# A prime-factor transform in place of the direct one, in a fused attention and long-convolution kernel

## The chip, the cores and the metric

The kernel runs on one NeuronCore of a Trainium2 chip. Such a core has five engines that run side by side, each with its own queue of instructions: TensorE (matrix products, here PE, with its weight loads PEld), VectorE (DVE), ScalarE (ACT), GpSimd (POOL) and SyncE (SP), which here only issues DMA transfers. The engines wait for each other by semaphores. Products land in PSUM, a small memory of eight banks of 512 fp32 words for each of 128 partitions; everything else lies in SBUF. The metric is the device time of one execution in microseconds (us).

## What is computed

Attention with a mask that differs by head, then a gated long convolution over the sequence, and a projection. Cut to what matters:

```python
B, H, S, D = 4, 8, 768, 64          # after attention: x is 4 x 768 x 512
scores = np.matmul(q, k.transpose(0, 1, 3, 2)) / 8
a = softmax(where(mask, scores, -1e9))   # heads 0, 2, 6: causal; the others: causal, and
                                         # the last 64 positions or the first 4 keys
x = (a @ v), heads side by side
proj = x @ w_proj                   # 512 -> 3 * 512
x1, x2, x3 = three parts of proj
X2 = rfft(x2, n=S); Hf = rfft(filter_fft, n=S)
y = x1 * irfft(X2 * Hf, n=S) * x3   # a circular convolution along the 768 positions
out = y @ w_out
```

The transform along the sequence is linear, so the kernel transforms the attention's output first and projects its spectrum with the middle third of w_proj. A real transform of 768 points has 385 frequencies; the kernel holds them as cosine and sine rows and computes all of it by matrix products with tables.

## The kernel before

**Tiling.** A pair of heads (128 columns of x) is one unit, n = 0 to 15; four pairs make a batch, b = 0 to 3. A sequence of 768 is six tiles of 128 positions.

**An order written out by hand.** Every step is a small function with a name, registered by `@op(name)`. The strings AHEAD and FAST list the names in the order in which they are issued; since each engine takes its instructions in order, the strings set the order on every engine. A name can carry an engine (`/v` VectorE, `/s` ScalarE, `/p` GpSimd, for copies and two-input steps that more than one can do) and a PSUM bank (`@0` to `@7`). Two helpers write these steps: `ev` (lines 969 to 975) copies, `two` (line 978) combines two operands; so in the profile most copies have one line and are told apart by their tiles.

**The steps of one pair n.** `lq`, `lk`, `lv` load; `cq`, `ck`, `cv` cast to bf16; `T`, `E` turn q and k (by TensorE and a copy for n below TURNED = 8, by a DMA transpose above); `kx`, `ks`, `vx`, `vs` gather the few keys and values that a windowed head needs; `sc` the scores (line 1452); `ex` the exponentials on ScalarE (line 1471, tile pT). The mask is added to the scores by TensorE, as a product of an identity with a table of large negative numbers, for n below BIASED_FAST = 4 (`sb`, line 1465), and multiplied into the exponentials by VectorE or GpSimd otherwise (`mk`, `mr`, table mtab). `at` multiplies with the values (line 1516), `rec` and `nm` divide (line 1533), into tile attn. `tn` and `te` turn attn into xT (channels on partitions), by TensorE for the pairs in TURNED_BACK and by a DMA transpose for the others.

**The forward transform of a pair.** `fd` and `fe` form the difference and the sum of the two halves of the sequence (tile fo): odd and even frequencies. For the pairs in SIXTHS (all of them) `fA`, `fS`, `fb`, `fr` split each half once more by three (tiles uv, br). `W{n}.{u}` (lines 1569 to 1573) is then three products for each u, of 256, 256 and 128 columns, into bank u; `We{n}` copies both banks (2 x 384 words) to xh.

**The filter.** Its columns are folded (`fold0`, `fold1`), transformed by `F` (line 1265, 18 products of 512 columns with the tables G and Gh) and scaled into HAB by `H` steps, with two DMA transfers `Hd` that move rows between partition halves. The tables come from one sine and one cosine over 384 columns (`sin`, `cos`), mixed by `skew` and `Gm` steps; the inverse table Gi is the forward table turned by TensorE (`Gt`, line 1227, and `Ge`).

**The middle, per batch b.** `X{b}.{t}.{u}` projects the spectrum (line 1620), `Xe` copies it out, `pa`, `pb`, `pc` multiply it with the filter as complex numbers into tile P (t = 0 to 2). For t = 2 the two DMA transfers `sw` swap partition halves first (tile Xw).

**The inverse and the gates, per block cb of 128 channels.** `x1` and `x3` project x itself (line 1655), `xs` copies x1 out, `g` multiplies with x3 straight from PSUM (line 1674; for the last cb line 1678) into tile gy. `c{b}.{cb}.{r}` is the inverse: for r = 0 and 1 three products of 384 columns (line 1685). `ce` copies the first to evs, `cv{b}.{cb}.0` and `.1` add and subtract the second (line 1696) into conv, 768 positions, and `y` multiplies conv into gy. `o` projects (line 1712), `oe` copies out, `st` stores: two tiles of 128 positions at a time (512 KB), one at a time in the last batch.

**Warm-up.** `blank` steps are products of zeros, in 13 places of the first part (BLANKS counts them).

The reuse of memory is set by hand too: a tile's tag says which it shares, and RAW gives sizes. A general version for other head patterns follows behind a branch that isn't taken.

Of the kernel before, what the change touches and what calls it, by code (L numbers as in the profile page):

```python
# [9 lines left out]
FP32 = mybir.dt.float32  # L10
# [111 lines left out]
lflag lk0 lq0 lk1 lq1 mblank want tcol fcol0 table sin0 fcol1 blank0@6 tfrac quarter mtab0 par turns other angle  # L122
ident mtab1 wrap size sin cos
# [3 lines left out]
ones1 ones2 mtab3 blank5@0 lq2 lk2 blank10@1 ck0/v skew0/s lv0 parb skew1/p G32/s T0.1@2 xp0 cq0/v lk3 blank6@3  # L127
mtab2 E0.1/v lv1 blank8@4 Gk1/s lv3 blank7@5 Gm00 btab G31/p blank1@6 ck1/v kz1 lq3 T0.0@7 lk4 alt blank3@0 Gm2
cq1/s G30/p Gh0 lq4 T1.1@1 Gm01 kz0 lv2 E0.0/s G00/v T1.0@3 G01/p Gm1 cq2/s lk6 E1.1/v sc0.1@4 sb0.1 lq6 ck2/p
sc0.3@6 ex0.1 Gh1 E1.0/v sc0.4@0 ones0 kx1/p sb0.4 lk5 sb0.3 T2.1@2 ex0.4 kz2 lk7 sc0.0@4 E2.1/v lq5 cv0/p sb0.0  # L130
Gt1@3 ex0.3 lq7 blank2@0 kx2/v Gt2@1 Gk0/p ex0.0 lv6 T2.0@2 ks1/p Ge2/v ck3/p sc0.2@6 Ge1/s E2.0/v sc1.2@4 sb1.2
lfilt sb0.2 T3.1@0 ex1.2 sc0.5@2 Gt0@1 ex0.2 cv1/v sc2.3@4 E3.1/v lv4 vx1/p sb0.5 ex0.5 sc1.0@6 lw2.1 Ge0/v
sb1.0 ks2/s vs1/v at0.0@2 lw2.0 ex1.0 at0.1 cq3/v lw0.1 T3.0@0 ex2.3 kx3/v sc1.1@6 rec0 lw1.1 sb1.1 nm0/v cv3/s
blank11@1 ex1.1 sc2.1@4 fe0/p sb2.1 tn0@1 cq4/v E3.0/s at1.0@2 lw0.0 blank9@6 ex2.1 ks3/v sc2.4@6 ck4/v at1.1
lw1.0 ex2.4 T4.0@0 T4.1@4 vs3/v E4.0/s te0/v lwo sc3.1@6 sb3.1 rec1 E4.1/s nm1/v fd0/p sc3.2@0 sb3.2 ex3.1 fe1/v
tn1@5 fS0/p ex3.2 sc3.0@2 fold0/v sb3.0 sc2.0@6 ex3.0 vx3/v fd1/v F0.0@4 fA0/v fA1/p F0.1@0 H0.0/s fS1/v fb0/p
sb2.0 fold1/v sc2.2@2 H0.1/s sb2.2 ex2.0 fb1/p te1/v F1.0@1 fr1 ex2.2 F2.1@4 fr0 cv2/v H1.0/s F2.0 lv5 vs2/v
vx2/p H0.2/v at2.0@6 H2.0/s at2.1 ck6/p sc4.0@2 H2.1/s rec2 Hd0 at3.0@0 nm2/v at3.1 H2.2/s lk9 rec3 fe2/p F1.1@6
nm3/v ex4.0 Hd1 T6.1@7 fd2/p H1.1/v sc4.5@4 sc4.4@0 ex4.5 tn2@2 fe3/v ex4.4 fd3/v tn3@3 te2/v sc4.2@4 te3/v
ex4.2 mk4.2/p W1.0@0 E6.1/v W1.1 blank4@2 We1/s ks6/v sc4.1@4 fS3/p blank12@3 ex4.1 fA3/v sc4.3@0 fr3 x10.3.0@2  # L140
fb3/p cq6/s mk4.0/v W0.0@4 W0.1 ex4.3 lq9 x10.3.1 ck7/v ck5/s x30.0.0@0 We0/v fS2/p lk10 kx6/s T7.1@7 cq5/p
xs0.3/s x10.0.1@4 H1.2/s fA2/v lq8 x10.0.0 fb2/v E7.1/s fr2 mk4.1/v W3.0@2 lk8 cq7/s T5.0@6 xs0.0/v ks7/p
x30.0.1 E5.0/s lq10 kx7/v W3.1 cv6/v T7.0@7 We3/s T5.1@4 vs6/v lv9 vx6/p g0.0 T6.0@5 E7.0/s W2.1@2 W2.0 E6.0/v
cv4/p E5.1/s x10.1.0@0 We2/v kx5/s ks5/p lv7 at4.0@6 sc5.1@4 cv5/s sc5.0@2 H2.3 at4.1 H2.4 ex5.1 lv8 vx5/p
x10.1.1 rec4 vs5/p nm4/v ex5.0 sc5.2@4 ex5.2 sc6.0@6 H2.5 sc6.3@2 mk5.1/v ex6.0 X0.0.1@4 mk5.0/v mk5.2/v ex6.3
X0.0.0 mk6.0/v fe4/v xs0.1/s fd4/v sc7.1@6 sc6.1@2 fS4/v Xe0.0/s fA4/v sc7.0@0 fr4 ex6.1 pa0.0/v at5.0@4 at5.1
fb4/v mk6.1/p ex7.0 X0.1.1@2 rec5 nm5/v X0.1.0 ex7.1 fe5/v mk7.0/v X0.2.1@0 cq8/s fd5/v mk7.1/v Xe0.1/s sc7.2@4
sc6.4@6 X0.2.0 fA5/p ex7.2 ck10/v sc6.2@2 pa0.1/v Xe0.2/s tn4@4 pb0.1/v tn5@5 ex6.2 sw0.1 W4.0@0 mk7.2/v W4.1
sw0.0 ck8/v x10.2.0@2 We4/s pc0.1/v T8 cq10/s mr6/v x30.1.0@0 mk6.2/v ck9/s x30.1.1 fS5/v pa0.2/v T10 ex6.4
x10.2.1 fb5/p g0.1 cv7/s at6.0@6 cq9/s vx7/v x30.2.1@0 te5/v xs0.2/s fr5 T9 x30.2.0 vs7/v cv8/s W5.1@2 pb0.2/v  # L150
W5.0 te4/s at6.1 lk12 pc0.2/v We5/s lq11 rec6 pb0.0/p g0.2 c0.1.0@5 cv9/s c0.0.0@4 lk13 nm6/v sc8.2@2 ce0.0/s
sc8.4@0 ex8.2 lv10 ce0.1/v c0.2.0@4 pc0.0/v sc8.1@6 ex8.4 lk11 sc8.0@2 ks10/v fe6/v c0.1.1@5 vx9/v ex8.0 lq13
vs9/v c0.0.1@0 cv0.1.1 c0.3.1@1 ks9/p ex8.1 lq12 cv0.1.0 kx9/p sc8.3@2 y0.1/v c0.3.0@5 ex8.3 lv11 cv0.0.1
mk8.0/p at7.1@6 ce0.3/s cv0.0.0 at7.0 lv12 sc8.5@2 cv0.3.1 ce0.2/s tn6@0 ex8.5 y0.0/v x30.3.0@4 kx10/s rec7
mk8.2/p cv0.3.0 nm7/s x30.3.1 te6/v sc10.3@2 mk8.1/v y0.3/v at8.0@0 fd6/v g0.3 fS6/p at8.1 ck13/p tn7@6 ex10.3
rec8 sc10.1@4 te7/v c0.2.1@7 fe7/p ex10.1 x11.0.0@2 fA6/v fd7/p cv0.2.0 x11.0.1 cv0.2.1 x11.3.1@4 fb6/p xs1.0/s
# [772 lines left out]
def patterned(tc, pools, pre, q, k, v, flags, n_sink, window, moe_w_proj, moe_filter_fft, moe_w_out, out):  # L929
# [912 lines left out]
```

## Time and profile before

| | us |
|---|---|
| three runs | 190.65, 190.84, 192.29 |
| median | 190.84 |
| the profiled execution | 190.27 |
| its span, first to last instruction | 188.4 |
| VectorE busy in the span | 161.2 |
| ScalarE busy in the span | 145.6 |
| GpSimd busy in the span | 69.0 |

The time of an execution is a little longer than the span of its profile. A line of the profile with groups gives the source line, engine and operation, what was written from what with its shape, the count, the busy time in us and the mean ns of one, and after the last bar the idle time of the engine just before them with what ended it. A chain of waits goes back from the last instruction, at each step to what released it. TensorE's granted clock was 0.985 of full speed in the mean. The DMA queues moved 34.01 MB, most of it before 124 us.

### The profile page before, as it was taken

How to read it: one execution, taken by the hardware profiler on the slowest of the kernel's cores; microseconds unless marked ns; L12 is line 12 of the kernel's file. 1: busy time of each engine (PE TensorE's matmuls, PEld its weight loads, DVE VectorE, ACT ScalarE, POOL GpSimd, SP SyncE). 2: the span in 40 equal slices, each digit the busy share in tenths (PEclk: the TensorE clock that was granted, in tenths of full speed). 3: DMA queues.
4: the chain of work that ended last, by engine and by line, in shares of the span. 5: the costliest groups of instructions: out<-in, count | busy, mean ns of one | idle time of the engine just before them, and what ended most of it. 6: DMA issues, size and time to landing. Idle time of an engine off the chain costs nothing.

```text
span 188.4 us, 4493 instructions
## 1 busy us (share of the span) xinstructions
PE 176.5 (94%) x1694; PEld 103.4 (55%) x1694; DVE 161.2 (86%) x329; ACT 145.6 (77%) x210; POOL 69.0 (37%) x103
## 2 busy tenths in 40 slices
PE   7879999989998999999999999999999999999970
PEld 2437664647745563575555656655657765555530
DVE  6887799789889999999989999999899996499810
ACT  5787899999999999988989999696977332426360
POOL 5874785554322224670250460700650630000000
PEclk9978999999999999999999999999999999999997
DMA  4999999999999999999999989982162002312074
GB/s 152 330 274 279 208 197 236 270 286 251 213 202 225 215 185 166 233 219 213 202 233 228 228 221 238 250 87 56 60 98 111 3 2 111 135 36 111 11 286 157
DMA packets 78955, 34.01 MB, mean 180 GB/s; under 512 B 68306, under 2 KB 75218, under 8 KB 78930
## 3 DMA queue, kind: packets, MB, share of 16 engines
q1 hardware_dynamic: 75986, 30.81, 73.9%
q0 software_dynamic: 2944, 2.88, 9.1%
q8 instruction: 14, 0.23, 0.5%
q14 instruction: 11, 0.09, 0.2%
HBM read 24.64 MB, written 6.29 MB: 164 GB/s over the span
## 4 chain that ended last, share of the span: by engine, by line
PE 66%; ACT 14%; DVE 6%; DMA 5%; issue 3%; POOL 2%; SPq 2%; DVEq 0%; ACTq 0%; POOLq 0%
PE space L1655 18%; PE space L1712 11%; PE space L1620 8%; PE space L1452 7%; PE space L1685 7%; PE space L1516 6%; ACT f_pT L1471 4%; DMA f_qkT<-f_qk_bf 3%; ACT f_HAB L1274 3%; DMA f_v_f<-in_v_dram 2%; PE space L1465 2%; ACT f_qk_bf L975 2%; SPq L1383 2%; PE space L1569 1%; PE space L1571 1%
## 5 line engine op out<-in xcount | busy, mean ns | idle before, releaser
L1471 ACT ACTIVATE f_pT<-space 128x1024 bf16<-128x1024 f32 (+3 forms) x68 | 58.8, 917 | 6.1 <-PE space L1465 1.9
L1655 PE MATMUL space<-f_xT,f_wproj 128*128 128x384 bf16 x256 | 47.9, 326 | 0.1
L1655 PEld LDWEIGHTS <-f_wproj 128*128 128x128 bf16 x256 | 24.0, 98 | 17.1 <-issue 1.0
L1712 PE MATMUL space<-f_wout,r_gy 128*128 128x512 bf16 x96 | 24.7, 379 | 0.0
L1452 PE MATMUL space<-f_qkT 64*128 64x128 bf16 (+3 forms) x248 | 22.6, 253 | 1.1 <-DVE f_attn L1533 0.5
L1620 PE MATMUL space<-f_wproj,f_xh 128*128 128x512 bf16 x96 | 22.7, 379 | 0.1
L1685 PE MATMUL space<-f_Gi,r_P 128*128 128x384 bf16 x96 | 19.0, 326 | 0.7 <-ACT f_evs L975 0.3
L978 DVE TENSOR_TENSOR f_pT<-f_pT,r_mtab 128x1024 bf16<-128x1024 bf16 (+3 forms) x33 | 18.5, 583 | 0.8 <-ACT f_pT L1471 0.6
L975 ACT COPY f_o<-space 128x1024 f32<-128x1024 f32 (+1 forms) x12 | 9.9, 836 | 11.3 <-PE space L1712 11.2
L1516 PEld LDWEIGHTS <-f_pT 128*128 128x128 bf16 x472 | 16.7, 97 | 3.6 <-issue 0.9
L1516 PE MATMUL space<-f_v_aug,f_pT 128*128 128x65 bf16 x392 | 17.9, 193 | 0.6 <-ACT f_X L975 0.5
L1452 PEld LDWEIGHTS <-f_qkT 64*128 64x128 bf16 x248 | 10.3, 94 | 13.1 <-issue 10.4
L978 POOL TENSOR_TENSOR f_uv<-f_fo 128x256 bf16<-128x256 bf16 x12 | 9.1, 766 | 21.1 <-DVE f_fo L978 15.8
L1696 DVE TENSOR_TENSOR f_conv<-f_evs,space 128x384 bf16<-128x384 f32 x32 | 16.1, 545 | 0.6 <-PE space L1685 0.3
L975 ACT CAST f_xh<-space 128x768 bf16<-128x768 f32 x14 | 11.2, 808 | 4.9 <-PE space L1573 4.6
L1620 PEld LDWEIGHTS <-f_xh 128*128 128x128 bf16 x96 | 9.0, 98 | 10.0 <-issue 0.4
L1712 PEld LDWEIGHTS <-r_gy 128*128 128x128 bf16 x96 | 9.0, 98 | 8.9 <-issue 0.4
L1533 DVE TENSOR_TENSOR f_attn<-space,f_rec 128x768 bf16<-128x768 f32 x14 | 13.4, 955 | 0.4
L1685 PEld LDWEIGHTS <-r_P 128*128 128x128 bf16 x96 | 8.8, 97 | 7.4 <-issue 1.1
L978 POOL TENSOR_TENSOR f_fo<-f_attn 128x384 bf16<-128x384 bf16 x11 | 10.4, 960 | 2.4 <-DVE f_attn L1533 1.9
L975 ACT CAST f_X<-space 128x1024 bf16<-128x1024 f32 x8 | 8.2, 1020 | 2.8 <-PE space L1620 2.7
L978 POOL TENSOR_TENSOR f_pT<-f_pT,r_mtab 128x512 bf16<-128x512 bf16 (+1 forms) x6 | 6.8, 1146 | 9.1 <-ACT f_pT L1471 9.1
(136 smaller groups left out, 345.7 us busy)
## 6 DMA issues: line engine op xcount, KB each, us to landing
f_v_f<-in_v_dram SPq DMA_DIRECT2D x32, 192.0 KB, 4.7
out_dram<-f_o SPq DMA_DIRECT2D x9, 512.0 KB, 3.1
r_qk_f<-in_k_dram SPq DMA_DIRECT2D x10, 192.0 KB, 4.4
r_qk_f<-in_q_dram SPq DMA_DIRECT2D x10, 192.0 KB, 5.0
r_qk_f<-in_k_dram SPq DMA_DIRECT2D x4, 384.0 KB, 11.3
r_qk_f<-in_q_dram SPq DMA_DIRECT2D x4, 384.0 KB, 6.1
f_qk_f<-in_q_dram SPq DMA_DIRECT2D x4, 384.0 KB, 5.8
f_qk_f<-in_k_dram SPq DMA_DIRECT2D x4, 384.0 KB, 6.6
```

The lines of the kernel that those rows point to most:

```text
L975: nc.scalar.copy(out=out, in_=in_)
L978: (nc.gpsimd if now["engine"] == "p" else nc.vector).tensor_tensor(out, a, b, op)
L1274: nc.scalar.activation(out=out_(), in_=in_(), func=AF.Copy, scale=w / S)
L1452: nc.tensor.matmul(sc[:, bank, col:col + 128 * cnt], lhsT=keys, rhs=qkT(n)[rows, 0, 128 * i:128 * (i + cnt)], start=(col == 0 or not biase ...
L1471: nc.scalar.activation(out=pT(n)[:, c, :, 0:w], in_=held[f"sc.{n}.{c}"][:, :, 0:w], func=AF.Exp, scale=SCALE)
L1516: nc.tensor.matmul(att[:, hh, 65 * i:65 * i + 65], lhsT=pT(n)[:, c, bank, col:col + 128], rhs=values, start=(z == 0), stop=(z == len(here) ...
L1533: nc.vector.tensor_mul(attn(n).rearrange("p i hh d -> p hh i d"), rows[:, :, :, 0:64], held[f"rec.{n}"][:, :, :, None].to_broadcast([128, ...
L1620: nc.tensor.matmul(ps[:, u, :], lhsT=xh(b)[:, cc, chain, 128 * part:128 * part + 128], rhs=wproj()[:, cc, DM:2 * DM], start=(cc == 0), sto ...
L1655: nc.tensor.matmul(ps[:, s, 0:HS], lhsT=wproj()[:, cc, part * DM + cb * 128:part * DM + (cb + 1) * 128], rhs=xT(b)[:, cc, s * HS:s * HS + HS],
L1685: nc.tensor.matmul(ps[:, 0, 0:HS], lhsT=P(b)[:, t, u, ch], rhs=Gi()[:, tile_no], start=(m == 0), stop=(m == 2))
L1696: fn(conv[:, half * HS:half * HS + HS], held[f"evs.{b}.{cb}"], held[f"c_ps.{b}.{cb}.1"][:, 0, 0:HS])
L1712: nc.tensor.matmul(ps, lhsT=gy(b)[:, cb, i * 128:(i + 1) * 128], rhs=wout()[:, cb, :], start=(cb == 0), stop=(cb == NC - 1))
```

## The change

The transform is computed as 3 by 256 instead: 768 is 3 times 256, and the two are prime to each other, so the positions and the frequencies can be numbered by remainders and no mixing factors are needed between a transform of length 3 and one of length 256.

- **Forward.** `fe`, `fd`, `fA`, `fS`, `fb`, `fr` stay, with other signs and slots. `W` keeps three products per u of 256, 256 and 128 columns, but u = 0 and 1 now go into the same banks: u writes the words 2f + u, that is every second word. `We` then copies one row of 768 contiguous words; xh is six groups of 128.
- **Tables.** G has six tiles instead of 18. One sine and one cosine over 512 columns (five index steps on GpSimd, `fcol0` to `fcol4`). The inverse tables Gi and Gj are written directly; the turns `Gt`, their copies `Ge`, and the mixing steps go.
- **Filter.** It takes the pairs' way, in four blocks of 128 columns: `fAF` to `frF`, the half spectra `K{cc}.{u}`, copies `Ke{cc}`, then 24 turns by TensorE (`F0` to `F2`) and the scalings `H` into HAB. No `Hd`.
- **Middle.** No `sw`. Behind `pc`, nine steps per batch do the length-3 part of the inverse: `qa`, `qs`, `qz`, `qb`, `qp`, `qm` (two inputs, 1024 elements) and `qh`, `qd`, `qr` (scalings; `qr` 2048 elements on one partition).
- **Inverse.** `c{b}.{cb}` is six products of 256 columns, two for each remainder of the position by three. `ce` and the two half combinations go. For batches 0 to 2 (DIRECT) `y` multiplies straight from PSUM; for batch 3 `cv` copies first.
- **Positions by remainder.** `xs` and `g` read x1 and x3 from PSUM with a step of three words, so that gy is sorted by remainder; a row tile of the output is then every third position, and `st` stores such rows.
- **Masks as biases** for n below 8 instead of 4. **TURNED_BACK** loses n = 14. **BLANKS** has 21 products instead of 29. A step `gate` on GpSimd reads one element of pair 3's load ahead of the filter's and the weights' loads.
- AHEAD and FAST are a new order, with new banks and engines.

The diff, cut to its core (the order strings are left out):

```diff
-SIXTHS = (0, 1, 2, 3, 4, 5, 6, 7, 8, 9, 10, 11, 12, 13, 14, 15)
-TURNED_BACK = (0, 1, 2, 3, 4, 5, 6, 7, 14, 15)
+TURNED_BACK = (0, 1, 2, 3, 4, 5, 6, 7, 15)
-BIASED_FAST = 4
+BIASED_FAST = 8
-BLANKS = (5, 2, 2, 2, 2, 2, 2, 2, 2, 2, 2, 2, 2)
+BLANKS = (5, 2, 2, 2, 2, 2, 2, 2, 2)
+DIRECT = ((0, 0), (0, 1), (0, 2), (0, 3), (1, 0), (1, 1), (1, 2), (1, 3), (2, 0), (2, 1), (2, 2), (2, 3))
...
+    def spectrum(ps, u, uv, br, ch):
+        woven = lambda bank, count: ps[:, bank, 0:2 * count].rearrange("p (f u) -> p u f", u=2)[:, u]
+        nc.tensor.matmul(woven(0, 256), lhsT=br[:, 1, u, ch], rhs=G()[:, 3 * u:3 * u + 2], start=True, stop=False)
+        nc.tensor.matmul(woven(0, 256), lhsT=uv[:, 2 * u, ch], rhs=Gk()[:, u], start=False, stop=True)
+        nc.tensor.matmul(woven(1, 128), lhsT=br[:, 0, u, ch], rhs=G()[:, 3 * u + 2], start=True, stop=True)
+
+    def taken(x, ps):
+        ev(x.rearrange("p g f -> p (g f)"), ps.rearrange("p a f -> p (a f)")[:, 0:S])
...
-            ev(xh(b)[:, hp], held[f"W_ps.{n}"][:, :, 0:HS])
+            taken(xh(b)[:, hp], held[f"W_ps.{n}"])
...
+    def classes(ps):
+        return ps[:, :, 0:HS].rearrange("p h (t s) -> p s h t", s=3)
...
+        @op(f"qa{b}")
+        def _(b=b):
+            two(SD(b)[:, 0:2], P(b)[:, 1], P(b)[:, 2], ALU.add)
+        @op(f"qs{b}")
+        def _(b=b):
+            two(SD(b)[:, 2:4], P(b)[:, 1], P(b)[:, 2], ALU.subtract)
+        @op(f"qr{b}")
+        def _(b=b):
+            scale(SD(b)[0:1], flat(b)[0:1, 2:6], 2.0)
+        @op(f"qh{b}")
+        def _(b=b):
+            scale(Y0(b), P(b)[:, 0], 0.5)
+        @op(f"qz{b}")
+        def _(b=b):
+            two(Y0(b), Y0(b), SD(b)[:, 0:4:3], ALU.add)
+        @op(f"qd{b}")
+        def _(b=b):
+            scale(SD(b)[:, 1:3], SD(b)[:, 1:3], 2.0 * KAPPA)
+        @op(f"qb{b}")
+        def _(b=b):
+            two(P(b)[:, 0], P(b)[:, 0], SD(b)[:, 0:4:3], ALU.subtract)
+        @op(f"qp{b}")
+        def _(b=b):
+            two(flat(b)[:, 2:4], P(b)[:, 0], SD(b)[:, 1:3], ALU.add)
+        @op(f"qm{b}")
+        def _(b=b):
+            two(flat(b)[:, 4:6], P(b)[:, 0], SD(b)[:, 1:3], ALU.subtract)
...
-            for r in range(2):
-                @op(f"c{b}.{cb}.{r}")
-                def _(b=b, cb=cb, r=r, ch=ch):
-                    ps = banks(f"c_ps.{b}.{cb}.{r}", count=1)
-                    for m, (t, u, tile_no) in enumerate(INVERSE[r]):
-                        nc.tensor.matmul(ps[:, 0, 0:HS], lhsT=P(b)[:, t, u, ch], rhs=Gi()[:, tile_no],
-                                         start=(m == 0), stop=(m == 2))
+            @op(f"c{b}.{cb}")
+            def _(b=b, cb=cb, ch=ch):
+                ps = banks(f"c_ps.{b}.{cb}").rearrange("p a f -> p (a f)")
+                for s, (re, im) in enumerate(POINTS):
+                    for c, rows in enumerate((re, im)):
+                        rhs = Gi()[:, c].rearrange("p a f -> p (a f)")[:, START[s]:START[s] + 256] if s else Gj()[:, c]
+                        nc.tensor.matmul(ps[:, 256 * s:256 * s + 256], lhsT=rows(b)[:, ch], rhs=rhs,
+                                         start=(c == 0), stop=(c == 1))
...
+                if (b, cb) in DIRECT:
+                    to = y if cb < NC - 1 else buf(f"conv.{b}.{cb}", [128, S], BF16, f"conv{cb % 2}")
+                    nc.vector.tensor_mul(to, held[f"c_ps.{b}.{cb}"].rearrange("p a f -> p (a f)")[:, 0:S], x)
```

More of the change, by code (lines that the diff above doesn't have):

```diff
@@ L140 @@
[L140 to L144, printed above, removed]
@@ L1168, in _ @@
         def _(c=c):
[L1169 to L1171 removed]
+            ev(G()[:, c:c + 4:3], waves()[:, c])
+        @op(f"Gk{c}")
         def _(c=c):
[L1173 to L1183 removed]
@@ L1199, in _ @@
     @op("alt")
     def _():
[L1201 to L1212 removed]
+        nc.vector.tensor_copy(out=G()[:, 2, 64:65], in_=sign())
@@ L1252, in _ @@
     def _():
[L1253 removed]
+        two(fold()[:, 0], filt()[:, 0:NM, :], filt()[:, NM:NT, :], ALU.add)
     @op("fold1")
     def _():
[L1257 to L1266 removed]
```

437 lines of the change are left out of this document (203 added, 234 removed).

## The prediction

> **What bounds the kernel now.** I read the page's busy shares and slices first, then the busy time in five stretches, then the chain of waits.
>
> ```profile
> span 188.4 us, 4493 instructions
> ...
> PE 176.5 (94%) x1694; PEld 103.4 (55%) x1694; DVE 161.2 (86%) x329; ACT 145.6 (77%) x210; POOL 69.0 (37%) x103
> ...
> PE   7879999989998999999999999999999999999970
> ...
> ACT  5787899999999999988989999696977332426360
> ...
> PE 66%; ACT 14%; DVE 6%; DMA 5%; issue 3%; POOL 2%; SPq 2%; DVEq 0%; ACTq 0%; POOLq 0%
> ```
>
> TensorE is busy 94% of the span, and its slices are nearly full from the fourth to the 39th; ScalarE's thin out after the 25th. The chain that ended last is TensorE for two thirds.
>
> ```profile
> core 0: us, PE busy (x) PEld busy (x) DVE busy (x) ACT busy (x) POOL busy (x), PEclk, DMA share, GB/s
> 0.00:20.00 20.00, 17.10 (x130) 8.79 (x131) 15.43 (x40) 14.76 (x22) 13.82 (x37) 0.91 0.95 260
> 20.00:55.00 35.00, 33.17 (x436) 21.52 (x435) 30.46 (x58) 34.21 (x45) 19.08 (x27) 1.00 1.17 233
> 55.00:124.00 69.00, 67.47 (x689) 39.42 (x688) 66.13 (x143) 64.20 (x100) 24.54 (x27) 1.00 1.14 214
> 124.00:160.00 36.00, 36.00 (x325) 22.11 (x323) 32.69 (x65) 21.88 (x31) 11.53 (x13) 1.00 0.27 67
> 160.00:188.40 28.40, 22.73 (x121) 11.51 (x118) 16.46 (x27) 10.60 (x15) 0.00 (x0) 0.96 0.34 122
> ```
>
> Columns: length, then busy us of TensorE, its weight loads, VectorE, ScalarE, GpSimd. From 20 to 55 us ScalarE is the full engine (34.21 of 35.00), and TensorE has 1.83 us free. From 55 to 124 us three engines are nearly full: TensorE lacks 1.53 us, VectorE 2.87, ScalarE 4.80. From 124 to 160 us TensorE is never idle, and VectorE has 3.31 us free.
>
> ```profile
> 68.63 5.61 DMA f_qkT<-f_qk_bf
> 75.41 0.94 DVE f_conv L1696 x2
> ...
> 83.19 4.58 PE space L1655 x28
> ...
> 177.55 5.19 PE space L1712 x24
> 182.77 0.59 ACT f_o L975
> ```
>
> This is the chain in order of time. After 75.41 us its steps of more than half a microsecond are all TensorE's, down to the last output copy. Its two dense runs give the pace: 28 products of 384 columns in 4.58 us are 164 ns each, 24 of 512 in 5.19 us are 216 ns, so 0.42 ns a column. A busy time of a product (379 ns for 512 columns) is latency and isn't what it costs in a stream.
>
> **TensorE's part of the change.**
>
> ```profile
> L1685 PE MATMUL space<-f_Gi,r_P 128*128 128x384 bf16 x96 | 19.0, 326 | 0.7 <-ACT f_evs L975 0.3 <-DVE f_conv L1696 0.2
> ...
> L1569 PE MATMUL space<-r_G,f_br 128*128 128x256 bf16 x32 | 8.7, 273 | 0.5 <-ACT f_pT L1471 0.3 <-ACT f_xh L975 0.2
> ...
> L1573 PE MATMUL space<-r_G,f_br 128*128 128x128 bf16 x32 | 7.0, 219 | 0.0
> ...
> L1465 PE MATMUL space<-f_btab,r_identity 128*128 128x128 bf16 (+2 forms) x33 | 6.5, 303 | 0.0
> ...
> L1265 PE MATMUL space<-r_gy,r_G 128*128 128x512 bf16 x15 | 3.9, 379 | 0.3 <-DVE f_attn L1533 0.3
> ...
> L1227 PE MATMUL space<-r_identity,r_G 128*128 128x128 bf16 x18 | 1.9, 251 | 0.0
> ```
>
> The inverse (L1685) keeps its 96 products but of 256 columns: 96 x 128 x 0.42 = 5.2 us less, 3.9 of them in batches 1 to 3, behind 75 us. The 18 turns of the table (L1227) go: 18 x 54 = 1.0 us. The filter's 18 products of 512 columns (L1265 and its sister) become eight half spectra of 256 + 256 + 128 columns (270 ns each) and 24 turns of 54 ns: 3.9 becomes 3.5 us. Pair n = 14 is turned by DMA, 6 x 54 = 0.3 us less; such a transfer took 5.61 us (chain above), and the new order has four X halves, three long and four short output parts and five half spectra between it and its first reader, by the pace above 7.6 us of products, so it costs nothing (at most that 5.61 if the cover were gone). Four more head pairs get their mask as a bias: the 33 products of L1465 (10 of 512 columns, 5 of 384, 18 of 128) come a second time, 2.15 + 0.81 + 0.97 = 3.9 us, between 20 and 75 us. Eight warm-up products of 512 columns fewer fill time that nothing else could use: nothing.
>
> Spectra keep the three products per half (L1569, L1573 and the one between), but every one writes each second fp32 word. With the filter there are 32 + 8 such halves, 270 ns each when packed. No row has a product that writes with gaps. The nearest rows read PSUM with gaps (f_qkT) and without (f_xT), 768 elements each:
>
> ```profile
> L971 DVE COPY f_qkT<-space 128x768 bf16<-128x768 bf16 x8 | 7.6, 950 | 0.9 <-PE space L1407 0.9
> ...
> L975 ACT COPY f_qkT<-space 128x768 bf16<-128x768 bf16 x8 | 6.2, 802 | 0.1
> ...
> L971 DVE COPY f_xT<-space 128x768 bf16<-128x768 bf16 x8 | 4.3, 550 | 0.6 <-PE space L1589 0.6
> ...
> L975 ACT COPY f_xT<-space 128x768 bf16<-128x768 bf16 x2 | 1.6, 808 | 0.0
> ```
>
> ScalarE loses nothing by the gaps (802 against 808 ns), VectorE takes 950 for 550, 1.73 times. So the factor lies between 1.0 and about 2. I take 1.73: VectorE's packed copy is the fast one of these rows (below 0.72 ns an element, ScalarE's above 1), and a product at 0.42 ns a word is nearer to it. Then a half costs 0.197 us more: 20 of them before 75 us (the filter's eight, pairs 0 to 5) 3.9 us, 20 behind it 3.9 us.
>
> By the Trainium skill (Advanced Engine Details and Errata, PSUM Cachelines) PSUM works in lines of two fp32 values and any non-contiguous pattern slows products significantly. Read as half pace that is an estimate of 5.4 us in each part in place of 3.9, and a sum 3.0 us higher. No run here shows a gapped write, so the trace neither agrees nor disagrees.
>
> **VectorE's part.**
>
> ```profile
> L978 DVE TENSOR_TENSOR f_pT<-f_pT,r_mtab 128x1024 bf16<-128x1024 bf16 (+3 forms) x33 | 18.5, 583 | 0.8 <-ACT f_pT L1471 0.6
> ...
> L1696 DVE TENSOR_TENSOR f_conv<-f_evs,space 128x384 bf16<-128x384 f32 x32 | 16.1, 545 | 0.6 <-PE space L1685 0.3
> ...
> L978 DVE TENSOR_TENSOR r_P<-r_P,f_m 128x1024 bf16<-128x1024 bf16 x12 | 8.2, 687 | 0.1
> ...
> L1674 DVE TENSOR_TENSOR r_gy<-r_x1s,space 128x768 bf16<-128x768 bf16 x8 | 7.5, 942 | 0.3 <-PE space L1655 0.3
> ...
> L978 DVE TENSOR_TENSOR r_gy<-f_conv,r_gy 128x768 bf16<-128x768 bf16 x10 | 5.7, 569 | 0.1
> ...
> L971 DVE COPY f_o<-space 128x1024 f32<-128x1024 f32 (+1 forms) x3 | 3.1, 1047 | 3.9 <-PE space L1712 3.8
> ```
>
> Gone are the 32 half combinations (L1696, 545 ns), 17.4 us, and eleven of its masks (583 ns), 6.4 us, all early. Three output copies (3.1 us) go to ScalarE. Twelve multiplications by the inverse now read PSUM: 942 in place of 569 ns, and three of them come from GpSimd. New per batch are six two-input steps on 1024 elements (687 ns) and three scalings, shared among three engines. The filter's folds come once, while the old table's mixing steps go; I take these as even. Behind 75 us that is: 24 combinations, -13.1; eight multiplications 7.5 for five at 2.8; 18 new steps, +12.4; three scalings at an estimated 0.6, +1.8; outputs -3.1. Sum +2.7 us. VectorE has 6.2 us free from 55 to 160 us, but in-order queues don't meet the free moments, so between 0 and 2.7 I take half, +1.3 on the path.
>
> **ScalarE, DMA, the rest.**
>
> ```profile
> L975 ACT CAST f_xh<-space 128x768 bf16<-128x768 f32 x14 | 11.2, 808 | 4.9 <-PE space L1573 4.6
> ...
> L975 ACT COPY f_evs<-space 128x384 f32<-128x384 f32 x14 | 6.8, 493 | 3.1 <-DVE f_conv L1696 2.2 <-PE space L1685 0.8
> ...
> L1274 ACT ACTIVATE f_HAB<-space 128x1024 bf16<-128x1024 f32 (+2 forms) x6 | 5.1, 888 | 0.1
> ```
>
> ScalarE loses 6.9 us of f_evs and 5.1 of filter scalings (L1274), and gets four filter spectra and four inverses to copy (8 x 0.81 = 6.5), two outputs and half of the scalings: no more than it had. The spectra "in one row" save nothing: f_xh from two pieces takes 808 ns, as the contiguous f_xT does. The eight swaps of X and two of the filter leave the SP queue; the output stores keep rows of 2 KB. The new wait of GpSimd on pair 3's load (`gate`) holds the filter and weight loads queued behind it; pair 3's load is issued near the list's start, and the scores of two pairs stand between, so nothing, or the rest of its landing if not. Reading PSUM by thirds (xs, g) costs ScalarE nothing by the f_qkT row, and VectorE is at 942 already.
>
> **The sum.** Before 75 us TensorE gets 3.9 + 3.9 - 1.0 - 0.4 = 6.4 us more. It has 2.90 + 1.83 = 4.7 us free up to 55, so +1.7 (between 0, if ScalarE still sets the pace, and 6.4). Behind 75 us: -3.9 - 0.3 + 3.9 = -0.3, and VectorE's +1.3. Together +2.7 us on the profiled execution's 190.27 (span 188.4): 193.0. The runs' median, 190.84, lies 0.57 above that execution, so the forecast is **193.5 us**.
>
> **Rivals.** First, gapped writes are free, as gapped reads are for ScalarE. Then the late part is -4.2 us on TensorE, its room for VectorE shrinks from 6.2 to 2.0, and VectorE's 2.7 overflow by 0.7: -3.5 if all is had, half of it (-1.8) if queues stall; early 2.5 us fit into the 4.7 free. Midway, -2.6: 188.2 us. For it: ScalarE's rows. Against: VectorE's.
>
> Second, GpSimd's scaling exposes the new serial chain. `qd` of batches 1 and 3 runs there.
>
> ```profile
> L978 POOL TENSOR_TENSOR f_m<-f_X,f_HAB 128x1024 bf16<-128x1024 bf16 x1 | 2.1, 2123 | 3.5 <-DVE r_P L978 3.5
> ...
> L1161 POOL TENSOR_SCALAR f_skew<-r_P 128x256 f32<-128x256 f32 x1 | 1.1, 1057 | 0.4 <-ACT r_P L1155 0.4
> ```
>
> A two-input step on 1024 elements takes 2.12 us, a scaling of 256 takes 1.06, so by elements up to 4.2 for 1024. In the last batch VectorE has a step, a gate product and a step (0.69 + 0.94 + 0.69 = 2.3 us) before it needs the result; `qm`, `qp`, the gate products and with them the last inverses queue behind. Up to 2.3 us nothing happens; at 4.2 it costs 1.9 on top of the forecast: 195.4.
>
> Third, the inverse doesn't get shorter, since something else than columns paces it (its weight loads, evictions): 3.9 us are not had, 197.4. Against it: 384 and 512 columns go by 0.42 ns a column alike.
>
> **How the numbers follow.** What a measurement here can tell from no change is about 1%, 188.9 to 192.7. Forecast 0.50, with a range of its own of 190.5 to 196.5 (early part 0 to 6.4, factor up to 2): 0.30 slower, 0.16 same, 0.04 faster. Free writes 0.30, as ScalarE's rows and VectorE's stand two to one at most: 0.22 faster, 0.07 same, 0.01 slower. GpSimd's scaling 0.15: 0.13 slower, 0.02 same. No shorter inverse 0.05, slower. Together faster 0.26, same 0.25, slower 0.49. The range 187.0 to 197.5 leaves out the low end of free writes, and the high end of the second and third cases: about 2 in 10.
>
> **What would show it.** Starts of the spectrum's products 109 ns apart for 256 columns mean free writes, 190 to 215 mean the forecast; the inverse's should come every 109 ns. GpSimd's `qd` of 2.3 us or more, with TensorE idle before the last inverse, means the second rival. TensorE's busy share between 20 and 75 us should rise towards full; VectorE's should stay above 95% from 55 to 160 us. The prediction is wrong if TensorE shows new idle time behind 124 us, or if the head up to the first projections takes several microseconds longer or shorter: I have costed the new order's head only by sums.

## The result and the profile after

| | changed kernel | kernel before |
|---|---|---|
| median of its runs | 204.81 us (204.10 to 207.50) | 190.75 us (190.39 to 192.29) |
| ratio, 95% interval | 1.0703 (1.0639 to 1.0766) | 1 |
| profiled execution, span | 207.5 us, 205.7 us | 190.27 us, 188.4 us |

The change costs 14.1 us. The forecast was 193.5 us, with 197.5 as the upper end: the direction was right, the size far off. The profiled execution is a disturbed one, 2.7 us above the median: it shows where time lies and is not read for the total, and the ratios here and below leave such executions out while the medians hold all.

From the page of the changed kernel: span, busy times, and the slices of TensorE, ScalarE and the granted clock.

```profile
span 205.7 us, 4479 instructions
...
PE 185.8 (90%) x1708; PEld 112.6 (55%) x1725; DVE 164.5 (80%) x307; ACT 148.7 (72%) x201; POOL 80.5 (39%) x109
...
PE   7779966999999999769999999999998999999980
...
ACT  5959998797747895989788989823997224573560
...
PEclk9999997699999999988999999999999999999998
```

TensorE's row has gaps that it did not have before (6 and 6 in the sixth and seventh slice, 7 and 6 in the 17th and 18th), and one slice behind each the clock's row falls, to 7 and 6, then to 8 and 8. The prediction's stretches had it at 1.00 from 20 to 160 us. The stretches of the prediction, in the same columns (length, then busy us of TensorE, its weight loads, VectorE, ScalarE, GpSimd, then the clock):

```profile
core 0: us, PE busy (x) PEld busy (x) DVE busy (x) ACT busy (x) POOL busy (x), PEclk, DMA share, GB/s
0.00:20.00 20.00, 16.18 (x125) 7.62 (x127) 15.17 (x36) 15.36 (x22) 15.75 (x39) 1.00 0.96 276
20.00:55.00 35.00, 31.07 (x375) 21.85 (x375) 26.64 (x50) 30.72 (x43) 15.29 (x22) 0.90 1.15 224
55.00:124.00 69.00, 64.95 (x644) 39.34 (x650) 60.81 (x114) 56.48 (x80) 29.96 (x32) 0.98 0.96 189
124.00:160.00 36.00, 34.56 (x303) 20.66 (x308) 33.29 (x61) 26.40 (x33) 10.41 (x10) 1.00 0.22 57
160.00:205.70 45.70, 39.04 (x269) 23.16 (x270) 28.59 (x48) 19.70 (x26) 9.10 (x8) 0.98 0.27 98
```

From 20 to 55 us nobody is busier than before: TensorE 31.07 us for 33.17, VectorE 26.64 for 30.46, ScalarE 30.72 for 34.21, and the clock is 0.90. So work is waiting for work. Behind 160 us 45.7 us are left where 28.4 were. Two of the prediction's signs of being wrong are there: from 124 to 160 us TensorE has 1.44 us of new idle time, and from 20 to 75 us its busy time falls from 51.96 to 50.57 of 55 us where it should have risen. VectorE's share from 55 to 160 us, which was to stay above 95%, was 94% before (98.81 of 105 us) and is 90% now (94.10).

Three rows decide between the cases of the prediction. First the starts of a spectrum's products, from the timeline (start, duration):

```profile
122.05 0.42 PE L1269 MATMUL space<-r_G,f_br 128*128 128x256 bf16 x1
...
122.27 0.42 PE L1270 MATMUL space<-f_Gk,f_uv 128*128 128x256 bf16 x1
...
122.48 0.31 PE L1271 MATMUL space<-r_G,f_br 128*128 128x128 bf16 x1
...
122.59 0.42 PE L1269 MATMUL space<-r_G,f_br 128*128 128x256 bf16 x1
```

From 122.05 to 122.27 and on to 122.48 are 0.22 and 0.21 us for a product of 256 columns, and 0.11 for the one of 128: by the unrounded starts 216 and 109 ns, where the kernel before has 109 and 56. The gapped write runs at half pace, not at the 1.73 times that I took from VectorE. (14 of the 40 first products of a half are followed after 173 to 175 ns, so that a half costs a little less than twice its 270 ns.) Then the inverse and the scalings, from the groups by shape:

```profile
L1710 PE MATMUL space<-f_Gi,r_P 128*128 128x256 bf16 x64 | 10.3, 282 | 1.1 <-DVE r_P L975 1.1
...
L1176 POOL TENSOR_SCALAR f_SD<-f_SD 128x1024 bf16<-128x1024 bf16 x2 | 5.5, 2773 | 22.2 <-DVE f_SD L1174 22.2
...
L1176 POOL TENSOR_SCALAR f_SD<-r_P 1x2048 bf16<-1x2048 bf16 x1 | 5.4, 5364 | 11.8 <-DVE f_SD L975 11.8
...
L1174 DVE TENSOR_SCALAR f_SD<-r_P 1x2048 bf16<-1x2048 bf16 x2 | 1.4, 682 | 0.1
```

The inverse's products of 256 columns come 109 ns apart by the records' starts where they run back to back, so the third rival falls. On GpSimd the scaling of 1024 elements takes 2.77 us, and `qr` of batch 0, which I had not priced there, 5.36 us for 2048 elements in one partition; VectorE does that one in 0.68. What it does to its surroundings, from the timeline:

```profile
79.72 5.36 POOL L1176 TENSOR_SCALAR f_SD<-r_P 1x2048 bf16<-1x2048 bf16 x1 [11.80 <-DVE f_SD L975]
...
82.41 1.17 DVE L975 TENSOR_TENSOR f_fo<-f_attn 128x384 bf16<-128x384 bf16 x1
...
85.12 0.69 DVE L975 TENSOR_TENSOR f_Y<-f_Y,f_SD 128x1024 bf16<-128x1024 bf16 x1 [1.55 <-POOL f_SD L1176]
...
87.23 0.34 DVE L975 TENSOR_TENSOR f_fo<-f_attn 128x384 bf16<-128x384 bf16 x1
...
87.64 0.38 PE L1710 MATMUL space<-f_Gj,f_Y 128*128 128x256 bf16 x2 [0.39 <-ACT f_pT L1483]
```

VectorE's next step on `f_Y` waits 1.55 us for it (its bracket), a step of 0.34 us (the one at 87.23) takes 1.17 while GpSimd works, and the inverse of batch 0 starts at 87.64.

### The profile page after: what moved, and what is told of

The parts are those of the page before. It is cut to its first block, busy times and chain, and to the rows that moved or that the text cites. A ratio compares the mean times of both kernels' runs of the same rounds, so it can differ in the third digit from the quotient of the medians.

```text
span 205.7 us, 4479 instructions
## 1 busy us (share of the span) xinstructions
PE 185.8 (90%) x1708; PEld 112.6 (55%) x1725; DVE 164.5 (80%) x307; ACT 148.7 (72%) x201; POOL 80.5 (39%) x109
## 5 line engine op out<-in xcount | busy, mean ns | idle before, releaser
L1683 PE MATMUL space<-f_xT,f_wproj 128*128 128x384 bf16 x256 | 46.3, 327 | 0.5 <-DVE r_gy L1702 0.4
L972 ACT COPY f_o<-space 128x1024 f32<-128x1024 f32 (+1 forms) x15 | 12.6, 846 | 7.1 <-PE space L1736 7.0
L972 ACT CAST f_xh<-space 128x768 bf16<-128x768 f32 x12 | 9.6, 799 | 10.6 <-PE space L1271 10.6
L970 POOL COPY f_v_x<-f_v_aug 64x520 bf16<-64x520 bf16 (+1 forms) x15 | 9.3, 626 | 15.2 <-DVE f_v_aug L968 10.8
L975 POOL TENSOR_TENSOR f_fo<-f_attn 128x384 bf16<-128x384 bf16 x12 | 12.0, 1011 | 8.1 <-DVE f_attn L1545 7.5
L1270 PE MATMUL space<-f_Gk,f_uv 128*128 128x256 bf16 x32 | 14.4, 449 | 0.0
L1176 POOL TENSOR_SCALAR f_SD<-f_SD 128x1024 bf16<-128x1024 bf16 x2 | 5.5, 2773 | 22.2 <-DVE f_SD L1174 22.2
L1269 PE MATMUL space<-r_G,f_br 128*128 128x256 bf16 x32 | 13.5, 422 | 0.0
L1477 PE MATMUL space<-f_btab,r_identity 128*128 128x128 bf16 (+2 forms) x62 | 11.8, 283 | 0.6 <-issue 0.6
L975 DVE TENSOR_TENSOR f_pT<-f_pT,r_mtab 128x512 bf16<-128x512 bf16 (+3 forms) x22 | 11.5, 540 | 0.6 <-ACT f_pT L1483 0.6
```

The lines of the kernel that those rows point to most:

```text
L972: nc.scalar.copy(out=out, in_=in_)
L975: (nc.gpsimd if now["engine"] == "p" else nc.vector).tensor_tensor(out, a, b, op)
L1269: nc.tensor.matmul(woven(0, 256), lhsT=br[:, 1, u, ch], rhs=G()[:, 3 * u:3 * u + 2], start=True, stop=False)
L1270: nc.tensor.matmul(woven(0, 256), lhsT=uv[:, 2 * u, ch], rhs=Gk()[:, u], start=False, stop=True)
L1477: nc.tensor.matmul(held[f"sc.{n}.{c}"][:, bank, 128 * at:128 * (at + width)], lhsT=identity(), rhs=btab()[:, what:what + width], start=Fal ...
L1683: nc.tensor.matmul(ps[:, s, 0:HS], lhsT=wproj()[:, cc, part * DM + cb * 128:part * DM + (cb + 1) * 128], rhs=xT(b)[:, cc, s * HS:s * HS + HS],
```

## The experiments

Theory A: the gapped writes' pace is the main cost. Theory B: GpSimd's steps between spectrum and inverse hold the chain. Theory C: the new order leaves TensorE idle in the head, which halves its clock. Theory D came later: what is left is lost at 75 to 85 us to VectorE's added steps. Ratios are to the kernel before on the same chip, with 95% intervals; where medians and ratios differ, the ratios are compared.

### Packed writes

```diff
-        woven = lambda bank, count: ps[:, bank, 0:2 * count].rearrange("p (f u) -> p u f", u=2)[:, u]
+        woven = lambda third, count: ps[:, u, 256 * third:256 * third + count]
...
-        ev(x.rearrange("p g f -> p (g f)"), ps.rearrange("p a f -> p (a f)")[:, 0:S])
+        ev(x.rearrange("p g f -> p (g f)").rearrange("p (f u) -> p f u", u=2),
+           ps[:, 0:2, 0:HS].rearrange("p u f -> p f u"))
```

> The changed kernel, but the spectra's products write consecutive words (each half into its own bank, 384 words), and the copy that empties PSUM weaves the two halves while it reads; the result in SBUF is the same. Theory A (the gapped writes' pace is the main cost): the products of 256 columns start 109 ns apart again in place of 216, 40 halves x 0.27 = 10.8 us of TensorE's stream go, and the time falls from 204.8 by 8 to 11 us, to 194 to 197. Theory B (GpSimd's steps of the inverse's preparation hold the chain) and theory C (the new order leaves TensorE idle in the head, which also halves its clock): TensorE already waits for others in the stretches concerned, so at most 4 us go, 201 or more. The copy that weaves should take ScalarE 0.80 us as before; if the gapped reading costs it, 0.2 to 0.8 us more for each of 20 copies.

Measured: 197.86 us, ratio 1.0345 (1.0249 to 1.0440), 7 us less than the changed kernel, a little short of A's 8 to 11. The starts of packed products, from the timeline of a later run with this edit, and the group of copies that now weave:

```profile
93.72 0.27 PE L1269 MATMUL space<-r_G,f_br 128*128 128x256 bf16 x1
93.83 0.27 PE L1270 MATMUL space<-f_Gk,f_uv 128*128 128x256 bf16 x1
93.94 0.22 PE L1271 MATMUL space<-r_G,f_br 128*128 128x128 bf16 x1
94.00 0.27 PE L1269 MATMUL space<-r_G,f_br 128*128 128x256 bf16 x1
```

```profile
L972 ACT CAST f_xh<-space 128x768 bf16<-128x768 f32 x12 | 9.5, 802 | 5.0 <-PE space L1271 3.2 <-DVE r_gy L1702 1.8
```

0.11, 0.11, 0.06: the pace is back, and ScalarE's copy takes 802 ns as ever, although it jumps between two banks at each word. So the copies had nothing to gain from the gapped writes. Seven of the 10.8 us of stream came out: theory A holds for half of the loss, and B and C, which allowed it 4 us, fall as sole causes.

### The same price in the other kernel

```diff
-                    nc.tensor.matmul(ps[:, u, 0:256], lhsT=br(n)[:, 1, u], rhs=G()[:, 3 * u:3 * u + 2, 0],
+                    nc.tensor.matmul(woven(0, 256), lhsT=br(n)[:, 1, u], rhs=G()[:, 3 * u:3 * u + 2, 0],
...
-            ev(xh(b)[:, hp], held[f"W_ps.{n}"][:, :, 0:HS])
+            ev(xh(b)[:, hp], held[f"W_ps.{n}"].rearrange("p a f -> p (a f)")[:, 0:S].rearrange("p (f u) -> p u f", u=2))
```

> The kernel before, with one edit: the spectra's three products per half write every second word of PSUM, the two halves woven over the same two banks, and the copy reads them back apart. Its order, inverse and everything else stay. Theory A: the products of 256 columns go from 109 to 216 ns between starts, 32 halves x 0.27 = 8.6 us more on TensorE, which is the bound: 190.8 + 6 to 9 = 197 to 200. Theories B and C: other engines' time covers it, at most 4 us more, below 195.

Measured: 198.64 us, ratio 1.0404 (1.0308 to 1.0501), so 7.7 us by the ratio and 8.5 by the medians, for 8.6 us of added stream at most (14 of its 32 first products were followed after 171 to 174 ns). Its groups of products and of copies:

```profile
L1572 PE MATMUL space<-f_Gk,f_uv 128*128 128x256 bf16 x32 | 13.5, 421 | 0.0
...
L975 ACT CAST f_xh<-space 128x768 bf16<-128x768 f32 x14 | 11.2, 798 | 10.8 <-PE space L1574 10.8
```

The latency of 421 ns was 272 in the kernel before; the copies are the same (798 for 808 ns). In an order where TensorE is the bound, the gap costs its stream in full or nearly so.

### The four steps off GpSimd

```diff
- ... qr0/p ... qd1/p ... qh2/p ... qd3/p
+ ... qr0/s ... qd1/s ... qh2/s ... qd3/s
```

> The changed kernel, but the four steps between spectrum and inverse that ran on GpSimd (qr of batch 0 with 2048 elements in one row, qd of batches 1 and 3, qh of batch 2) run on ScalarE at the same place of the list. Theory B: TensorE's idle time between 80 and 90 us (3.1 us) and its half clock behind it go, 3 to 6 us faster, 199 to 202. Theory A: below 2 us, since the products' pace stays. Theory C: below 2 us.

Measured: 202.78 us, ratio 1.0637 (1.0541 to 1.0734). That is 2.0 us by the medians and 1.3 by the ratios (whose intervals overlap), where A and C had it and not the three to six of B. With the packed writes added:

> Both edits together. Theories A and B: the gains add up, 189 to 194, at or a little above the kernel before. Theory C: it stays at 195 or above, and TensorE's clock in the profile is still low between 30 and 40 us.

Measured: 195.53 us, ratio 1.0221 (1.0109 to 1.0334), half a microsecond on C's side, and the low clock between 30 and 40 us was there too (0.83, then 0.50). The timeline of this run shows what the steps do on ScalarE:

```profile
76.67 1.90 ACT L1178 ACTIVATE f_SD<-r_P 1x2048 bf16<-1x2048 bf16 x1
76.83 0.87 PE L1464 MATMUL space<-f_qkT 64*128 64x512 bf16 x4
...
78.48 1.69 ACT L1483 ACTIVATE f_pT<-space 128x1024 bf16<-128x1024 f32 x2
...
79.53 0.61 PE L1464 MATMUL space<-f_qkT 64*128 64x512 bf16 x4 [1.84 <-ACT f_pT L1483]
```

`qr` takes 1.90 us ahead of the exponentials (78.48), and TensorE waits 1.84 us for them (its bracket). So the step was moved to VectorE, where it takes 0.68:

> Packed spectra as before, and the four steps that ran on GpSimd are on VectorE in place of ScalarE. On ScalarE the scaling of 2048 elements in one row took 1.90 us ahead of five exponentials, and TensorE stood still for 2.2 us for them (77.2 to 79.4 us); on VectorE the same step takes 0.68 us, one of 1024 elements 0.43. Theory B (these steps' place and duration matter): TensorE's idle time and half clock at 75 to 85 us go, 195.5 becomes 191 to 194. Theory C (the head, 25 to 40 us, is what is left): the time stays within 1 us of 195.5.

Measured: 192.48 us, ratio 1.0114 (1.0021 to 1.0208). Repeated:

> The run with packed spectra and VectorE's steps once more, beside these two on the same chip, for its interval against the kernel before: 1.005 to 1.015 if 192.5 was right.

194.55 us, ratio 1.0145 (1.0094 to 1.0197); both agree on 1.013. The placement of four small steps was worth 2.1% (1.0345 to 1.013, 4 us). The same edit with the gapped writes left in:

> The changed kernel with its gapped writes, and the four steps on VectorE in place of GpSimd. With packed writes that edit was worth 5.4 us (197.9 to 192.5). Theories A and B as two costs that add up: 204.8 becomes 198.5 to 200.5. If the gapped products hide the steps' waits or feel them more: above 201 or below 198.

Measured: 202.31 us, ratio 1.0577 (1.0532 to 1.0621). By the ratios the steps are worth 1.3% beside gapped writes and 2.1% beside packed ones, and packing 3.6% with the steps on GpSimd and 4.5% (8.5 us) with them on VectorE. That looks as if each loss hid a part of the other, but the intervals together are wider than the difference of 0.9%: the two costs may as well simply add, and this is not shown either way.

All twelve scalings on VectorE (four more than before), together with the extra products of the next test:

> As the run with the nine extra products, and all scalings between spectrum and inverse (qr, qd, qh of every batch) on VectorE, none left on ScalarE (1.04 us for 1024 elements there, 1.90 for the row of 2048; 0.43 and 0.68 on VectorE). Theory B, carried on: another 0.5 to 2 us less, the tail's chain above all. Against it: VectorE is nearly full between 55 and 160 us, so 0 to 1 us more.

193.94 us, ratio 1.0182 (1.0075 to 1.0289), beside 1.0109 without the move: no gain, the sign unclear.

### The clock and the head

```diff
-BLANKS = (5, 2, 2, 2, 2, 2, 2, 2, 2)
+BLANKS = (5, 2, 2, 2, 2, 2, 2, 2, 2, 3, 2, 4)
...
- ... sc4.1@6 ... sc4.3@2 ... sc4.4@6
+ ... blank9@1 sc4.1@6 ... blank10@1 sc4.3@2 ... blank11@1 sc4.4@6
```

> As the run with packed spectra and VectorE's steps, plus nine products of 512 columns of zeros on TensorE, into a bank that nothing uses then, before three of the six scores of pair 4 (28 to 34 us), where TensorE waits for ScalarE's exponentials. They are 1.9 us of work more. Theory C1 (the idle time there makes the clock halve, and the half clock costs 2 to 3 us in the 5 us behind it): the granted clock stays at 1.00 between 30 and 40 us and the time falls by 2 to 3.5 us. Theory C2 (ScalarE sets the pace there, the clock only follows): the clock stays up and the time changes by less than 1 us. Were the idle time no cause of the clock, it would be slower by up to 1.9.

Measured: 193.33 us, ratio 1.0109 (0.9983 to 1.0235), no change that an interval of 2.4 us to either side can show. Stretches without and with the extra products:

```profile
core 0: us, PE busy (x) PEld busy (x) DVE busy (x) ACT busy (x) POOL busy (x), PEclk, DMA share, GB/s
...
30.00:35.00 5.00, 3.38 (x30) 1.79 (x30) 4.96 (x9) 5.00 (x8) 3.81 (x6) 0.87 1.16 269
35.00:40.00 5.00, 4.87 (x57) 3.73 (x58) 3.92 (x7) 4.88 (x7) 1.62 (x3) 0.79 1.19 221
```

```profile
30.00:35.00 5.00, 4.11 (x35) 1.85 (x35) 4.92 (x8) 4.49 (x7) 3.97 (x6) 1.00 1.16 268
35.00:40.00 5.00, 4.00 (x45) 2.59 (x44) 4.06 (x7) 4.84 (x9) 3.71 (x6) 1.00 1.17 253
```

The clock goes from 0.87 and 0.79 to 1.00 and 1.00 as C1 said, and the time stays, as C2 said. These are one profile of each; the table below shows that the clock also stayed up once without the products. In both, ScalarE is busy 9.3 us or more of these ten. So three of its copies were moved:

```diff
- ... te0/s ... cq6/s ... cv3/s
+ ... te0/v ... cq6/v ... cv3/v
```

> As the run with packed spectra and VectorE's steps (192.5), with three copies of the head moved from ScalarE to VectorE at the same place of the list: the turned pair 0 (0.92 us), the cast of pair 6's queries (0.96) and of pair 3's values (0.97). ScalarE is full from 20 to 40 us there (10.0 us of each 10), VectorE has 2.7 us free. Theory C in the form that the extra products left (ScalarE's queue, and not TensorE's clock, sets the head's pace): the fold of the head ends 1 to 2.5 us sooner and the time falls by as much, to 190 to 191.5. If the head is not what the rest waits for, or VectorE's new waits for the loads cost as much: within 0.7 us.

193.08 us, ratio 1.0128 (1.0070 to 1.0187): nothing. With one doubling more:

> As the run before, and the doubling of batch 0 (qd, 1.09 us on ScalarE between the exponentials and the normalizing of pair 7, with VectorE waiting for its result) moves to VectorE (0.43 us). If ScalarE still sets the pace at 75 to 83 us, 0.5 to 1 us less than without it; if VectorE does, the same or 0.4 more.

192.40 us, ratio 1.0123 (1.0071 to 1.0176): nothing again.

The traces hold a cause that none of these runs tried. Five of the runs with packed writes have the same code up to 70 us, and yet the head's length differs between their profiles. As a mark of it I take the start of the fourth `rec` on VectorE. GpSimd's cast of the keys of pair 7 waits for its load in most of them, and GpSimd's later steps wait behind it:

| profile of the run | the cast starts (its wait for the load) | clock, 30 to 35, 35 to 40, 40 to 45 us | fourth `rec` starts |
|---|---|---|---|
| sixteen steps left out (last experiment) | 25.60 (none) | 1.00, 1.00, 1.00 | 44.86 |
| four steps on VectorE | 27.84 (2.23) | 0.87, 0.79, 1.00 | 45.20 |
| its repeat | 30.00 (4.38) | 0.86, 0.80, 1.00 | 45.49 |
| four steps on ScalarE | 28.28 (2.67) | 0.83, 0.50, 0.99 | 46.79 |
| steps of pair 6 on GpSimd (below) | 30.37 (4.75) | 0.89, 0.50, 0.92 | 47.43 |

In the first row the clock stays at 1.00 without any extra products, although TensorE's idle stretches up to 33 us are those of the second row (0.72, 0.89, 0.41 and 0.7 us). So it is not shown that the nine products were what held it up. Between the first three rows the low clock goes with 0.3 to 0.6 us; where it stays at 0.50 for five microseconds the mark comes 1.9 to 2.6 us later. Whether the clock or a late load does that, no run separates. In the kernel before, no step waits for a load by more than 0.3 us between 20 and 50 us.

### Masks by multiplication

`BIASED_FAST` back to 4: the `sb` products of pairs 4 to 7 go, and their `mk` and `mr` steps stand on VectorE some five places behind the exponential they need.

> As the run with the nine extra products, but pairs 4 to 7 get their masks as in the kernel before, by multiplications on VectorE behind the exponentials (13 of them, 0.55 us or less each) and not as products on TensorE. If the bias products cost what the prediction gave them (3.9 us on TensorE between 20 and 75 us), it is 2 to 4 us faster. If VectorE or its waits for the exponentials set the pace, it is 1 to 6 us slower.

Measured: 199.94 us, ratio 1.0480 (1.0369 to 1.0590), 3.7% slower. The group of mask multiplications without and with the edit (line 975 is 973 there):

```profile
L975 DVE TENSOR_TENSOR f_pT<-f_pT,r_mtab 128x512 bf16<-128x512 bf16 (+3 forms) x22 | 11.7, 545 | 0.3 <-ACT f_pT L1483 0.2
```

```profile
L973 DVE TENSOR_TENSOR f_pT<-f_pT,r_mtab 128x512 bf16<-128x512 bf16 (+3 forms) x35 | 19.6, 571 | 4.1 <-ACT f_pT L1481 4.1
```

Thirteen multiplications are 7.9 us more of VectorE, and its wait for exponentials ahead of them goes from 0.3 to 4.1 us. The bias products are the cheap way; how much of the 3.7% is the place that I gave the steps was not tried.

### What is left: 75 to 85 us

```diff
- ... fe6/v ... qd0/s fd6/v ... nm7/s ... fS6/v fA6/v
+ ... fe6/p ... qd0/v fd6/p ... nm7/v ... fS6/p fA6/p
```

> As the run with packed spectra and VectorE's steps (192.5), with the stretch from 75 to 85 us relieved, where VectorE is busy 10.0 of 10 us, ScalarE 9.5 and GpSimd 2.3: four small steps of pair 6 go from VectorE to GpSimd, the doubling of batch 0 (1.09 us) and the normalizing of pair 7 (2.60 us) from ScalarE to VectorE (0.43 and 0.95). By the records TensorE has done 16.9 us of products between 75 and 95 us there, against 19.2 in the kernel before. Theory D (what is left above the kernel before is lost in this stretch): 1 to 2.5 us less, 190 to 191.5, level with the kernel before. If it is lost in the head, within 0.7 us of 192.5.

Measured: 196.63 us, ratio 1.0369 (1.0325 to 1.0414), 4 us slower in place of 1 to 2.5 faster. VectorE's three steps there, first in the run without the edit, then with it and with GpSimd's:

```profile
78.08 0.67 DVE L975 TENSOR_TENSOR f_Y<-f_Y,f_SD 128x1024 bf16<-128x1024 bf16 x1
78.69 0.67 DVE L975 TENSOR_TENSOR r_P<-r_P,f_SD 128x1024 bf16<-128x1024 bf16 x1
79.29 0.54 DVE L968 CAST f_qk_bf<-f_qk_f 128x768 bf16<-128x768 f32 x1
```

```profile
78.53 1.78 POOL L975 TENSOR_TENSOR f_fo<-f_attn 128x384 bf16<-128x384 bf16 x2 [0.53 <-DVE f_attn L1545]
...
80.03 0.82 DVE L975 TENSOR_TENSOR f_Y<-f_Y,f_SD 128x1024 bf16<-128x1024 bf16 x1
...
80.38 2.07 POOL L975 TENSOR_TENSOR f_uv<-f_fo 128x256 bf16<-128x256 bf16 x2
...
80.77 1.15 DVE L975 TENSOR_TENSOR r_P<-r_P,f_SD 128x1024 bf16<-128x1024 bf16 x1
...
81.85 1.02 DVE L968 CAST f_qk_bf<-f_qk_f 128x768 bf16<-128x768 f32 x1
```

The same three steps take 0.67, 0.67 and 0.54 us without GpSimd beside them, and 0.82, 1.15 and 1.02 with it. What was taken off VectorE came back, at least in part, as slower steps: 1.1 us on these three. Of the 3.2 us between the two profiles 2.2 lie ahead of 75 us, where their code is the same (second and last row of the table above), so how the loss of 4 us comes about is shown for about 1 us only.

> As the run with packed spectra and VectorE's steps (192.5), leaving out four in-place steps of batch 0 between spectrum and inverse (qr, qz, qb, qd: 0.68 + 0.69 + 0.69 us of VectorE and 1.09 of ScalarE), so batch 0's output is not the reference's. Theory D (VectorE's added steps hold the path at 75 to 85 us, where TensorE gets 2.3 us behind the kernel before): 1.5 to 2.5 us less, 190 to 191. Otherwise (the loss lies elsewhere, or these steps lie beside other work): within 0.7 us.

Measured: 191.68 us, ratio 1.0103 (1.0057 to 1.0150). The same four steps left out of all batches:

> The same four steps left out of all four batches. Theory D in its narrow form (only batch 0 stands in a stretch where VectorE sets the pace; behind 95 us TensorE is full): no more than 0.7 us beyond the run that leaves them out of batch 0, and up to 1 us of the last batch's chain. The prediction's term (VectorE's added work behind 75 us, half on the path) would give another 1.3 to 2.7 us.

Measured: 191.65 us, ratio 1.0060 (1.0014 to 1.0106). Against the 1.0145 of the repeat, on the same chip, 0.8 us go with batch 0's steps and 0.8 with the other three batches'; the intervals overlap, so the sizes are rough. Neither is what was expected: theory D had 1.5 to 2.5 us for batch 0, and the prediction's term 1.3 to 2.7 us for the others. Theory D holds for a part at most, and even with sixteen steps left out (thirteen of VectorE's, three of ScalarE's) it is no faster than the kernel before.

## Why the prediction was wrong

**Gapped writes: the mechanism was right, the size too small, and its cover wrong.** The term said 1.73 times, 3.9 us early and 3.9 late, the early part mostly into free time of TensorE. The factor is 2.0: 5.4 and 5.4. The step that failed with it is the choice of VectorE's row ("a product at 0.42 ns a word is nearer to it"): a read by another engine is no row for a write by TensorE. The Trainium skill (Advanced Engine Details and Errata, PSUM Cachelines) had the rule, lines of two fp32 values and significantly slower products for any pattern that is not contiguous; the traces agree, with 216 ns for 109. The prediction had even reckoned half pace, 5.4 us in each part, and did not take it. On the time it was 7 us by packing (8.5 with the second cost gone) and 7.7 in the kernel before: most of it went through, where the sum had let 4.7 us of early work vanish in TensorE's free time. The first rival (free writes, 0.30) had no ground but ScalarE's rows.

**The scalings: the second rival's mechanism, at a step I did not look at.** The sum has three scalings "at an estimated 0.6", VectorE's share of those behind 75 us, and nothing for the others, while the order gives four of the twelve to GpSimd. I bounded only `qd` of the last batch (2.1 to 4.2 us). It measured 2.77, and there, where the rival looked, TensorE waited no more than 0.41 us. `qr` of batch 0 costs 5.36 us at 80 us, in the middle of the kernel, where I had VectorE full and so nothing to hide a wait. Moving four steps was worth 2.4 us (gapped) to 4 us (packed), with overlapping intervals; the rival gave 1.9 for its one place.

**The inverse** gets shorter as said (109 ns for 256 columns), so the late gain of 3.9 us is real in the stream. **ScalarE** got a little more to do where "no more than it had" was said: 148.7 busy us for 145.6, and 147.2 with packed writes and the four steps on VectorE. Its copies take 0.80 us each, as said.

**VectorE's added steps, half of 2.7 us on the path.** Leaving out four of the nine steps a batch, about 8.4 us of VectorE's work and 4.0 of ScalarE's, gave 0.8% in all, 1.6 us. So little of this work lies on the path, which is the side that the term took. Its size is not tested by that: the 2.7 us are what is left of new steps against the combinations that went, and no run takes out that difference alone.

**The head, +1.7.** This step was mis-sized, and it is the one whose cause stays partly open. Summed by columns at 0.42 ns, the warm-up products left out, TensorE had 124.1 us of products ahead of it at 55 us in the kernel before and 124.0 in the packed version with VectorE's steps, although the latter's inverse and pair 14 are 5.5 us shorter behind that point (5.2 and 0.3), against 2.2 us of the added bias products that still stand there: the head had left some 3.2 us of work undone. I had counted TensorE's free time there as room (4.7 us), but work arrives only as ScalarE and VectorE finish exponentials, copies and folds. Nor were VectorE's 6.4 us of masks without worth: taking the bias products back costs 3.7%. Three copies of ScalarE's are not what holds the head. Late loads and a low clock go with a longer one in some executions (the mark at 47.4 in place of 44.9 us), but the profile with neither has 2.4 to 3.3 us of work undone as well (a range, since a few products are missing from its records). What causes that was not found; neither a head in the old order with the new inverse nor an earlier load of those keys was tried.

The account of the loss, in ratios: 1.070 to 1.0345 by the pace of the writes, to 1.013 by four steps on the wrong engine, to 1.006 by further steps of VectorE that cannot simply be left out, and 0.6% open. No version here beats the kernel before.

## What to carry to other kernels

Price an operation by a row of its own engine and its own access, and where there is none, take the whole width as likely: a gapped read by one engine says nothing on a gapped write by another. When a list places steps by hand, price every one on the engine it stands on, single-partition ones too: 2048 elements in one partition cost GpSimd about twice what 1024 in each of 128 do. Free time of an engine in one stretch is room only for work that is ready then.

## What the runs showed that I had not expected

- A write to every second fp32 word of PSUM halves TensorE's pace (216 for 109 ns), while ScalarE reads words from two banks in turn at no cost (802 ns).
- VectorE's steps on SBUF slow down by 1.2 to 1.9 times while GpSimd works beside them (0.82 for 0.67 us, 1.02 for 0.54), and a step of 0.34 us took 1.17 during GpSimd's 5.36 us. The Trainium skill (SBUF — State Buffer, Who interferes with whom) has these two share a port pair that one of them holds for a whole instruction; the trace agrees in the direction, its steps being stretched by 0.15 to 0.8 us, but not in the length: that step of 1.17 us ended at 83.58, while GpSimd's instruction ran to 85.08.
- The granted clock fell to 0.50 behind a stretch in which TensorE was busy for 3.4 of 5 us and never idle for more than 0.9 us, and it did not fall in another execution with the same idle stretches. With nine products of zeros, 1.9 us, it was at 1.00, and no time was gained.
